# Clearing the sign on ScalarE instead of VectorE in a weight conversion, with the clamp's bounds in the other order

## The chip, the cores and the metric

One Trainium2 chip, one of its cores. The metric is the device time of one execution in microseconds. A profile of one execution gives the instruction times used below. In it PE is TensorE (PEld its weight loads), DVE is VectorE, ACT is ScalarE, POOL is GpSimd and SP is SyncE, whose queue issues the DMAs. Each engine works off one list of instructions in its order, so an instruction that waits holds up all that stand behind it on that engine.

## What is computed

A recurrence over 768 time steps for 4 x 8 heads of size 40, and then two gated feed-forward layers over the 3072 rows that it gives. Cut to what matters here:

```python
for t in range(S):                                   # S = 768
    y[:, :, t] = einsum('bhd,bhde->bhe', rt, state)
    Sa = einsum('bhde,bhe->bhd', state, at)
    state = state * wt[:, :, None, :] - einsum('bhd,bhe->bhde', Sa, bt) + einsum('bhd,bhe->bhde', vt, kt)
x = y.transpose(0, 2, 1, 3).reshape(3072, 320)
g = x @ w_gate;  x = (g * sigmoid(g) * (x @ w_val)) @ w_out          # layer 1
out = (sigmoid(x @ w2_gate) * (x @ w2_val)) @ w2_out                  # layer 2
```

The six weight matrices (320 x 1536 or 1536 x 320) come to the kernel as 64-bit floats. Their conversion to a pair of 32-bit floats, a high part and a rest, is what is changed.

## The kernel before

**The attention part** (`attention`, lines 43 to 677) takes the time axis in 12 chunks of 64 steps. For each chunk `prep_a` builds scaled keys, `prep_b` solves small triangular systems on VectorE (lines 409 to 423) with a round trip through DRAM, and `chain` and `post` carry the state on and form the output. Several chunks are in work at once; `merge` interleaves these generators by rates and due times written at lines 635 to 645.

**The feed-forward part** (`Ffn`) cuts the hidden size of 1536 into 12 slices of 128 (index f). For one slice `load_w` converts the weights and `gate` uses them: 16 TensorE matmuls per block of 256 rows (line 809), a sigmoid on ScalarE (813), one or two products on VectorE (815, 816), the split of the result into a rounded high part on ScalarE (817) and a rest on GpSimd (818); `add` then makes 6 matmuls more (827). The rows come in 12 blocks.

**The order of the stages.** Some slices of layer 1 are converted and used while attention still runs (`more` and `extra`, lines 1016 to 1041). After attention the remaining slices of layer 1 run over all blocks, and during that time the 12 slices of layer 2 are converted (`load_w2`, called from `each1`, line 1081). Then layer 2 runs from weights that are all there. The program's text is not the order on the engines: the kernel is built with `schedule_with_timeline_sim=True` (line 1186), so a planner writes each engine's order from its own estimate of when each instruction is ready.

**One conversion** (`load_w`, lines 699 to 736) is done three times for a slice (twice with 384 columns, once with 320), 72 times in all. A DMA brings the 64-bit words into `raw`, of which `lo` and `hi` are the even and odd 32-bit words, so both are read with a step of 8 bytes. The steps on `dt` (called `t` in the code) and `ds` (`sg`):

- 707, VectorE: `dt` = `hi` without its sign bit
- 708, GpSimd: clamp of `dt` as a 32-bit float
- 711 and 712, VectorE: two shifts, then sign and top bit of `hi` put back
- 716 and 717, VectorE: scale from the exponent bits, then times `lo`
- 727, ScalarE: rounded high part of the weight
- 729, GpSimd: `dt` minus the high part; 731, 733 or 735, GpSimd: plus `ds`, into the low part

While attention runs there is at first one `raw`, one `dt` and one `ds`; in its last chunks a second set joins, and after it there are three `raw` and two each of `dt` and `ds`.

Of the kernel before, what the change touches and what calls it, by code (L numbers as in the profile page):

```python
# [9 lines left out]
F32 = mybir.dt.float32  # L10
# [3 lines left out]
AF = mybir.ActivationFunctionType  # L14
ALU = mybir.AluOpType
# [23 lines left out]
F_LOW = 2.0**-15  # L39
F_HIGH = (1.875 - 2.0**-23) * 2.0**16  # L40
# [639 lines left out]
class Ffn:  # L680
# [7 lines left out]
    def load_w(self, pool, tag, layer, f):  # L688

        nc = self.nc  # L690
        w8 = pool.tile([P, 11 * P + 2 * DM], F32R, tag=tag, name="w8")
        wh, wl = w8[:, 0 : 6 * P + DM], w8[:, 6 * P + DM :]
        for n in range(3):
            sz = 3 * P if n < 2 else DM
            at = 3 * P * n
            (p0, t0), (p1, t1), (p2, t2) = self.raw[self.n % len(self.raw)]
            self.n += 1
            raw = p0.tile([P, 3 * P, 2], I32, tag=t0, name="raw")
            nc.sync.dma_start(
                out=raw[:, 0:sz].rearrange("p f w -> p (f w)"), in_=layer[0][f, :, 2 * at : 2 * at + 2 * sz]  # L700
            )
            lo, hi = raw[:, 0:sz, 0], raw[:, 0:sz, 1]
            t = p1.tile([P, 3 * P], I32, tag=t1, name="dt")[:, 0:sz]
            sg = p2.tile([P, 3 * P], I32, tag=t2, name="ds")[:, 0:sz]
            ts = nc.vector.tensor_scalar

            ts(out=t, in0=hi, scalar1=0x7FFFFFFF, scalar2=None, op0=ALU.bitwise_and)  # L707
            nc.gpsimd.tensor_scalar(  # L708
                out=t.bitcast(F32), in0=t.bitcast(F32), scalar1=F_LOW, scalar2=F_HIGH, op0=ALU.max, op1=ALU.min
            )  # L710
            ts(out=t, in0=t, scalar1=5, scalar2=2, op0=ALU.logical_shift_left, op1=ALU.logical_shift_right)  # L711
            nc.vector.scalar_tensor_tensor(  # L712
                out=t, in0=hi, scalar=-(1 << 30), in1=t, op0=ALU.bitwise_and, op1=ALU.bitwise_or
            )

            ts(out=sg, in0=t, scalar1=-(1 << 23), scalar2=None, op0=ALU.bitwise_and)
            nc.vector.scalar_tensor_tensor(  # L717
                out=sg.bitcast(F32),
                in0=lo.bitcast(U32),
                scalar=2.0**-52,  # L720
                in1=sg.bitcast(F32),
                op0=ALU.mult,
                op1=ALU.mult,
            )
            tf, pf = t.bitcast(F32), sg.bitcast(F32)
            w = wh[:, at : at + sz]
            nc.scalar.copy(out=w, in_=tf)  # L727
            sub = nc.gpsimd.tensor_tensor
            sub(out=tf, in0=tf, in1=w.bitcast(F32), op=ALU.subtract)  # L729
            if n < 2:  # L730
                sub(out=wl[:, 2 * P * n : 2 * P * n + 2 * P], in0=tf[:, 0 : 2 * P], in1=pf[:, 0 : 2 * P], op=ALU.add)
                g = slice(64 * n, 64 * n + 64)
                sub(out=wl[g, 4 * P : 5 * P], in0=tf[g, 2 * P :], in1=pf[g, 2 * P :], op=ALU.add)
            else:
                sub(out=wl[:, 5 * P :], in0=tf, in1=pf, op=ALU.add)
            yield
        self.w = wh, wl
# [452 lines left out]
```

## Time and profile before

| | |
|---|---|
| time, median of 3 runs | 1460.96 us (1457.96 to 1463.65) |
| span of the profiled execution | 1462.6 us |
| busy share of the span | PE 88%, PEld 83%, DVE 59%, ACT 37%, POOL 46% |
| granted TensorE clock, mean | 0.890 of full speed |
| ending chain, by engine | PE 43%, DVE 30%, DMA 10%, POOL 5%, SP's queue 5%, issue 5%, ACT 1% |

The page gives the profiled execution by its span alone. The span lies within the three timed runs, 0.1% above their median, so a difference worked out in the span is applied to the median as it stands. The busy share says how much of the span an engine was executing, not whether the end waited for it. The chain is followed back from the last instruction, at each step to what released it; its shares say what the end waited for.

### The profile page before, as it was taken

The page shows a single profiled execution, that of the slowest core. Times are in us where ns is not written, and L with a number is a line of the kernel's source. Part 1 is how long each engine was busy: PE and PEld are TensorE (multiplying, and loading weights), DVE is VectorE, ACT ScalarE, POOL GpSimd, SP SyncE. Part 2 cuts the span into 40 slices and gives each one's busy share as a digit, 9 for nine tenths or more (in the row PEclk, how much of TensorE's full clock was granted, in tenths as well). Part 3 has the DMA queues.
Part 4 walks back from the last instruction along what each step waited for, and adds up shares of the span by engine and source line. Part 5 has one row for each costly group of instructions (what it writes and reads, how often), then busy time and mean ns, then how long its engine had stood idle before and what let it go on. Part 6 is the DMA issues. An engine that isn't in the chain of part 4 may idle for free.

```text
span 1462.6 us, 32637 instructions
## 1 busy us (share of the span) xinstructions
PE 1282.7 (88%) x13197; PEld 1207.8 (83%) x13197; DVE 858.1 (59%) x1644; ACT 535.1 (37%) x1260; POOL 678.0 (46%) x800
## 2 busy tenths in 40 slices
PE   4548867789899899887979999999999999999996
PEld 4447756678888888786979988889999999999996
DVE  8679759388756865876687999886311122112111
ACT  5223524253445444533433332333333333333331
POOL 4378468352213222245587888996222222222221
PEclk7556858696989999886999999999999999999998
DMA  5854884946355446425234654442100000100000
GB/s 139 206 114 107 170 195 94 187 97 159 88 125 140 102 119 147 93 62 132 87 99 155 185 164 132 140 135 95 63 21 21 21 21 22 30 21 21 12 13 17
DMA packets 242096, 144.49 MB, mean 99 GB/s; under 512 B 186768, under 2 KB 218512, under 8 KB 241552
## 3 DMA queue, kind: packets, MB, share of 16 engines
q1 hardware_dynamic: 241936, 142.31, 37.6%
q8 instruction: 106, 1.74, 0.5%
q14 instruction: 54, 0.44, 0.1%
HBM read 104.00 MB, written 38.27 MB: 97 GB/s over the span
## 4 chain that ended last, share of the span: by engine, by line
PE 43%; DVE 30%; DMA 10%; POOL 5%; SPq 5%; issue 5%; ACT 1%; POOLq 0%; DVEq 0%; ACTq 0%
PE g L809 21%; PE po L827 11%; DVE pr L417 7%; PE gv L809 4%; DVE part L423 4%; DMA sn<-nd 3%; DVE dt L712 3%; DVE dt L711 2%; POOL dt L708 2%; SPq L219 2%; DVE ds L717 2%; DMA raw<-in_w_dram 2%; DVE g L815 1%; PE kps L364 1%; DVE dt L707 1%
## 5 line engine op out<-in xcount | busy, mean ns | idle before, releaser
L809 PE MATMUL g<-x,w 128*128 128x256 f32 x3552 | 495.3, 284 | 12.8 <-DVE g L815 11.8
L809 PEld LDWEIGHTS g<-x,w 128*128 128x128 f32 x3552 | 462.8, 190 | 19.0 <-DVE g L815 16.7
L818 POOL TENSOR_TENSOR hl<-g,hh 128x256 fp32r<-128x256 f32 x288 | 220.5, 768 | 452.8 <-ACT hh L817 409.5
L816 DVE TENSOR_TENSOR g<-g,g 128x256 f32<-128x256 f32 x222 | 93.7, 422 | 307.7 <-PE g L809 297.7
L827 PE MATMUL po<-w,hh 128*128 128x320 f32 x1152 | 230.0, 314 | 2.8 <-ACT hh L817 1.4
L817 ACT CAST hh<-g 128x256 fp32r<-128x256 f32 x288 | 117.0, 406 | 302.8 <-DVE g L816 276.4
L809 PE MATMUL gv<-x,w 128*128 128x256 f32 x1056 | 173.4, 318 | 30.4 <-DVE g L816 18.2
L809 PEld LDWEIGHTS gv<-x,w 128*128 128x128 f32 x1056 | 152.9, 217 | 38.2 <-DVE g L816 24.2
L827 PEld LDWEIGHTS po<-w,hh 128*128 128x128 f32 x1152 | 179.0, 191 | 4.6 <-ACT hh L817 2.6
L417 DVE TENSOR_TENSOR pr<-part,sn 128x4 f32<-128x4 f32 (+4 forms) x180 | 150.1, 834 | 4.0
L827 PE MATMUL po<-w,hl 128*128 128x320 f32 x576 | 145.1, 318 | 2.9 <-POOL hl L818 2.9
L813 ACT ACTIVATE g<-g 128x256 f32<-128x256 f32 x222 | 85.1, 384 | 142.5 <-PE g L809 109.4
L708 POOL TENSOR_SCALAR dt<-dt 128x384 f32<-128x384 f32 (+1 forms) x72 | 109.2, 1519 | 40.9 <-DVE dt L707 38.0
L729 POOL TENSOR_TENSOR dt<-dt,w 128x384 f32<-128x384 f32 (+1 forms) x72 | 79.3, 1101 | 78.4 <-ACT w L727 32.3
L827 PEld LDWEIGHTS po<-w,hl 128*128 128x128 f32 x576 | 93.8, 191 | 5.2 <-POOL hl L818 4.2
L423 DVE TENSOR_REDUCE part<-pr 128x2 f32<-128x4 f32 (+4 forms) x180 | 88.9, 494 | 4.0
L364 PE MATMUL kps<-lq,kbt 104*128 104x128 f32 x384 | 69.4, 338 | 18.6 <-DVE lq L374 15.6
L364 PEld LDWEIGHTS kps<-lq,kbt 104*128 104x128 f32 x384 | 61.8, 244 | 23.2 <-issue 13.2
L727 ACT CAST w<-dt 128x384 fp32r<-128x384 f32 (+1 forms) x72 | 35.6, 495 | 98.6 <-DVE dt L712 91.5
L570 PE MATMUL aps<-rbd,ut 104*128 104x128 f32 x384 | 61.5, 307 | 9.3 <-DVE ysb L607 3.0
L707 DVE TENSOR_SCALAR dt<-raw 128x384 int32<-128x384 int32 (+1 forms) x72 | 44.9, 624 | 40.2 <-DMA raw<-in_w_dram 34.1
L372 ACT ACTIVATE bn<-kps 64x256 f32<-64x256 f32 x96 | 36.4, 379 | 84.5 <-PE kps L364 46.6
(129 smaller groups left out, 1762.1 us busy)
## 6 DMA issues: line engine op xcount, KB each, us to landing
raw<-in_w_dram SPq DMA_DIRECT2D x48, 384.0 KB
xd<-x SPq DMA_DIRECT2D x12, 896.0 KB
x<-xd SPq DMA_DIRECT2D x12, 896.0 KB
raw<-in_w_dram SPq DMA_DIRECT2D x24, 320.0 KB
pn<-pd SPq DMA_DIRECT2D x46, 160.0 KB
ld<-in_a_kb_dram SPq DMA_DIRECT2D x22, 320.0 KB
ld<-rd SPq DMA_DIRECT2D x44, 160.0 KB
sn<-nd SPq DMA_DIRECT2D x24, 256.0 KB
```

What stands on the lines that cost most here:

```text
L364: nc.tensor.matmul(kps[:, n].rearrange("p h t -> p (h t)"), lhsT=kbt[0:PW, n, :], rhs=lq[m % 3][0:PW, 4 * g4 + n].rearrange("p h t -> p (h ...
L417: nc.vector.tensor_tensor(out=o, in0=xs[:, 0:kk, None, 0:n].to_broadcast([P, kk, 2, n]), in1=sn[:, None, 0:n, n : n + 2].rearrange("p o s ...
L423: nc.vector.tensor_reduce(out=xs[:, 0:kk, n : n + 2], in_=o, axis=AX.X, op=ALU.add)
L570: nc.tensor.matmul(aps[:, n, h2], lhsT=ut[0:PW, x, 2 * h2 : 2 * h2 + 2].rearrange("p u s -> p (u s)"), rhs=rbd[0:PW, x, h2].rearrange("p b ...
L708: nc.gpsimd.tensor_scalar(out=t.bitcast(F32), in0=t.bitcast(F32), scalar1=F_LOW, scalar2=F_HIGH, op0=ALU.max, op1=ALU.min)
L729: sub(out=tf, in0=tf, in1=w.bitcast(F32), op=ALU.subtract)
L809: nc.tensor.matmul(gv[n], lhsT=p, rhs=q, start=e == 0, stop=e == len(seq) - 1)
L813: nc.scalar.activation(out=g, in_=gv[0], func=AF.Sigmoid)
L816: nc.vector.tensor_tensor(out=g, in0=gv[1], in1=g, op=ALU.mult)
L817: nc.scalar.copy(out=hh, in_=g)
L818: self.heng.tensor_tensor(out=hl, in0=g, in1=hh.bitcast(F32), op=ALU.subtract)
L827: self.nc.tensor.matmul(ops[u], lhsT=p[:, us], rhs=q, start=first and n == 0, stop=last and n == 2)
```

## The change

One line of the conversion and the arguments of the next are altered:

```diff
-            ts(out=t, in0=hi, scalar1=0x7FFFFFFF, scalar2=None, op0=ALU.bitwise_and)
+            nc.scalar.activation(out=t.bitcast(F32), in_=raw.bitcast(F32)[:, 0:sz, 1], func=AF.Abs)
             nc.gpsimd.tensor_scalar(
-                out=t.bitcast(F32), in0=t.bitcast(F32), scalar1=F_LOW, scalar2=F_HIGH, op0=ALU.max, op1=ALU.min
+                out=t.bitcast(F32), in0=t.bitcast(F32), scalar1=F_HIGH, scalar2=F_LOW, op0=ALU.min, op1=ALU.max
             )
```

`ts` is VectorE's `tensor_scalar`. The sign of `hi` is now cleared by an absolute value on ScalarE, which reads the same 32-bit words as floats, with the same step, and writes the same tile. The clamp on GpSimd has the same two operations on the same data in the other order. Nothing else of the text changes; the planner writes the order on the engines anew.

## Rows read from the trace of the kernel before

**Rows 1.** The page of the profile, its head.

```profile
span 1462.6 us, 32637 instructions
```

**Rows 2.** Stretches: us, each engine's busy us (instructions), granted TensorE clock, DMA share, GB/s.

```profile
0.00:330.00 330.00, 224.74 (x2623) 196.96 (x2624) 242.75 (x428) 126.91 (x266) 188.59 (x211) 0.69 0.64 145
...
620.00:720.00 100.00, 87.27 (x1218) 78.13 (x1213) 62.08 (x127) 36.58 (x85) 46.34 (x55) 0.83 0.36 88
720.00:860.00 140.00, 127.46 (x1155) 120.92 (x1155) 122.56 (x261) 46.44 (x118) 111.51 (x122) 1.00 0.46 146
860.00:1005.00 145.00, 132.77 (x996) 128.37 (x995) 130.16 (x230) 45.74 (x116) 131.23 (x141) 0.99 0.42 137
1005.00:1462.60 457.60, 445.90 (x3517) 444.86 (x3515) 96.15 (x219) 146.36 (x375) 126.11 (x185) 0.99 0.09 26
```

**Rows 3.** Waits of TensorE, 860 to 1005 us: total us, times, longest.

```profile
PE g L809 <- DVE g L815: 10.4, 11, 2.0
PE po L827 <- POOL hl L818: 1.7, 3, 0.6
```

**Rows 4.** The chain of waits, by line: 0:330, 620:720, 720:860, 860:1005, in that order.

```profile
by line: DVE pr L417 12.0%; SPq L219 7.8%; DMA sn<-nd 5.9%; DVE part L423 5.4%; issue 5.0%; DMA pn<-pd 3.5%; PE gv L809 3.1%; DVE lq L374 2.8%; DVE wp L183 2.8%; DMA ld<-in_a_kb_dram 2.4%; DMA raw<-in_w_dram 2.4%; SPq L443 2.0%; DMA pd<-wp 
...
by line: PE gv L809 13.3%; DVE pr L417 9.8%; DMA raw<-in_w_dram 9.6%; DVE part L423 6.6%; PE po L827 5.9%; DMA xs<-ob 4.6%; DMA xd<-part 4.5%; DMA sn<-nd 4.2%; PE yps L596 4.0%; DMA nd<-bn 3.7%; issue 3.4%; PE aps L570 3.1%; DVE dt L707 2.3
...
by line: issue 10.7%; DVE dt L712 7.9%; DVE dt L711 7.1%; DVE wacc L1115 6.5%; DVE g L815 5.5%; POOL dt L708 5.3%; DVE g L816 5.3%; DVE ds L717 5.2%; DMA wt<-in_a_w_dram 5.2%; DVE wacc L1114 5.1%; POOL dt L729 4.7%; DVE dt L707 4.2%; DMA ra
...
by line: DVE dt L712 14.5%; issue 14.4%; POOL dt L708 10.5%; DVE dt L711 9.8%; DVE ds L717 6.9%; POOL hl L818 5.8%; DVE g L815 5.3%; DVE dt L707 5.1%; DVE ds L716 5.1%; POOL dt L729 4.8%; POOL w L731 4.6%; DVE g L816 4.2%; POOL w L733 2.9%;
```

**Rows 5.** Stretches as in group 2, for line 707 alone.

```profile
0.00:330.00 330.00, 5.95 (x15) 0.69 0.64 145
...
620.00:720.00 100.00, 4.57 (x9) 0.83 0.36 88
720.00:860.00 140.00, 11.78 (x22) 1.00 0.46 146
860.00:1005.00 145.00, 21.53 (x25) 0.99 0.42 137
```

**Rows 6.** Line 707, whole span: durations ns min/median/max; its waits; who waited for it.

```profile
L707 DVE TENSOR_SCALAR dt<-raw x72: 309/411/2056, 84.2 to 999.5; 128x384 int32<-128x384 int32 x48, 128x320 int32<-128x320 int32 x24
...
  DMA raw<-in_w_dram: 34.1, 12
...
  POOL dt L708: 38.0, 38
```

**Rows 7.** VectorE, 862 to 869 us in order of time: start us, us.

```profile
863.13 2.06 DVE L707 TENSOR_SCALAR dt<-raw 128x320 int32<-128x320 int32 x1
...
866.08 0.36 DVE L707 TENSOR_SCALAR dt<-raw 128x384 int32<-128x384 int32 x1
866.93 0.62 DVE L711 TENSOR_SCALAR dt<-dt 128x320 int32<-128x320 int32 x1 [0.49 <-POOL dt L708]
```

**Rows 8.** GpSimd in the same stretch.

```profile
863.57 0.73 POOL L818 TENSOR_TENSOR hl<-g,hh 128x256 fp32r<-128x256 f32 x1
864.27 0.73 POOL L731 TENSOR_TENSOR w<-dt,ds 128x256 fp32r<-128x256 f32 x1
```

**Rows 9.** ScalarE groups by shape: xcount, busy us, mean ns, idle before.

```profile
L727 ACT CAST w<-dt 128x384 fp32r<-128x384 f32 x48 | 24.6, 512 | 64.2 <-DVE dt L712 57.2 <-PE yps L596 5.1 <-POOL w L735 1.8
...
L465 ACT COPY zt<-zps 32x512 f32<-32x512 f32 x24 | 14.9, 619 | 18.5 <-PE zps L455 18.2
...
L427 ACT COPY xt<-part 128x512 f32<-128x512 f32 x12 | 13.2, 1103 | 11.4 <-DVE part L423 11.4
...
L81 ACT ACT_TABLE_LOAD x1 | 1.3, 1283 | 0.8 <-PEq L1178 0.8
L813 ACT ACT_TABLE_LOAD x1 | 1.3, 1283 | 0.0
```

**Rows 10.** What line 813 waited for on ScalarE, 860 to 1005 us.

```profile
  POOL hl L818: 20.8, 18
```

## The prediction

> **What bounds the kernel now.** The profiled execution spans 1462.6 us [rows 1]. I read the busy times by stretch first [rows 2]. From 1005 us on TensorE is busy 445.9 of 457.6 us: layer 2 is a pure TensorE stage, has no conversions, and nothing of this change can reach it. From 720 to 1005 us TensorE is busy 260.2 of 285 us (127.46 + 132.77) at a granted clock of 0.99 to 1.00, while VectorE is busy 252.7 us and GpSimd 242.7 us of the same 285. All three are nearly full, and what TensorE loses there is 24.8 us. The waits of TensorE in the last 145 us name the cause: it stands for VectorE's line 815, and a little for GpSimd's 818, 12.1 us in all [rows 3]. Before 720 us the picture is that of attention: TensorE has gaps everywhere, and the chain goes through the triangular solves on VectorE and through DMAs [rows 4].
>
> Line 707 was read next. Of its 72 runs 47 lie between 720 and 1005 us, and there it takes 33.3 us of VectorE; 9 lie in 620 to 720 us (4.6 us) and 15 before 330 us (6.0 us) [rows 5]. Its duration is uneven: 309 ns at best, 411 in the median, 2056 at worst [rows 6]. In the busiest stretch the mean is 21.53 / 25 = 0.86 us [rows 5]. Then the chain of waits by stretch [rows 4]: line 707 has 2.3% of 100 us, 4.2% of 140 us and 5.1% of 145 us, which is 2.3 + 5.9 + 7.4 = 15.6 us of the way to the end. That is 41% of the 37.9 us for which it is busy in these three stretches. In the first 330 us it is not among the lines listed, so under 2.0%, or 6.6 us; I leave it out of the sum.
>
> **What the change removes.** 72 VectorE instructions, of which 15.6 us stand on the chain. If nothing took their place, that is the gain. But some of the length of line 707 is not its own work. A clean run over 384 columns took 0.36 us, while one over 320 columns took 2.06 us; during it GpSimd ran lines 818 and 731, and line 707 ended 0.2 us after the second of them [rows 7, 8]. So part of what is measured as line 707 is time in which it stood beside GpSimd. The next VectorE instruction on SBUF data, 711 or 712, may stand in its place. With clean runs alone, 56 x 0.36 us = 20.2 us of the 37.9 us would be freed, and by the same 41% the chain loses 8.3 us, not 15.6.
>
> The Trainium skill bears on that (GPSIMD Engine Reference, section "Key points"): GpSimd shares its SBUF interfaces with VectorE and collides with VectorE instructions in a two-port mode or with two SBUF inputs. The trace agrees as far as the stretched run goes. By that rule the lost time goes to the next such VectorE instruction, and the gain is the smaller of the two figures above.
>
> **What it adds.** 72 absolute values on ScalarE. The trace has none. The nearest row is the cast of the same tile, 128 x 384, at 512 ns [rows 9]; it reads without a step, while the new one reads every second word. A ScalarE copy with a step of two words on its output (32 x 512) took 619 ns, one that reads with a step of 32 words (128 x 512) took 1103 ns [rows 9]. Scaled by columns the last is 1103 x 384 / 512 = 827 ns. So the bounds are 512 and 827 ns; I take 512, because a step of two words is nearer to the 619 ns row, which is hardly above what the cast gives for 512 columns (512 x 512 / 384 = 683 ns). In all 72 x 0.51 = 37 us of ScalarE, at most 60. ScalarE is busy 46.4 of 140 and 45.7 of 145 us [rows 2], so 47 of them, 24 to 39 us, fit into 193 idle us.
>
> Where the clamp on GpSimd waits for the cleared word, the new instruction stands on the path: 38 of 72 times today [rows 6]. Of the 56 conversions in the three stretches that makes 30, and by the same 41% 12.3 are on the chain: 12.3 x 0.51 = 6.3 us come back, or 10.2 us at 827 ns.
>
> The Trainium skill speaks against the change (ScalarE: Activation LUTs, "Rules for kernel authors"): simple elementwise work belongs on VectorE, which is faster per element. For the clean runs the trace agrees, 0.36 against 0.51 us; the runs beside GpSimd at a mean of 0.86 us go the other way. By the rule alone each conversion becomes 0.15 us longer, by the stretched rows it becomes shorter.
>
> **What it moves.** Line 707 is the first to touch `raw`, and VectorE stood 34.1 us in 12 waits for its DMA [rows 6]. In the chain that DMA has 2.4% of 330 us and 9.6% of 100 us, 7.9 + 9.6 = 17.5 us [rows 4]. These waits go to ScalarE's list. VectorE is then free for its solves (417, 423), but held up instead are ScalarE's copies of transposed tiles and sigmoids (360, 349, 813, 817), for which TensorE waits. Line 711 still needs the whole way over DMA, ScalarE and GpSimd. So the bounds are a gain of 17.5 us (what is on the chain vanishes) and a loss of 34.1 - 17.5 = 16.6 us (what was harmless on VectorE gets onto the path on ScalarE). I take zero, between the two. The new instruction also has to wait until GpSimd has let go of the previous `dt`. No DMA is added; the release of `raw` still hangs on line 717. The other order of the clamp is two operations for two, and costs nothing: GpSimd passes over the same columns in one instruction.
>
> **The sum.** -15.6 + 6.3 + 0 = -9.3 us against the span of 1462.6 us [rows 1], or against the median: 1460.96 - 9.3 = 1451.7. I predict 1452 us.
>
> **The rivals.** About 0.5% (7.3 us) is what a measurement of this kernel can tell from no change: its three runs spread over 5.7 us.
>
> *GpSimd keeps the pace.* From 860 to 1005 us it is busy 131.2 of 145 us [rows 2], its load is unchanged, and the sigmoid already waits 20.8 us for its line 818 [rows 10]. Then relieving VectorE only turns VectorE's work into VectorE's idle time. With the smaller relief of 8.3 us and 6.3 us coming back, the gain is 2.0 us, and with a little off in the earlier stretch some 3: 1458 us. Against it: GpSimd had 13.8 us idle there, so it is not quite full.
>
> *ScalarE is held up (the slower one).* The waits for `raw` and for the previous `dt` block ScalarE in front of the copies and sigmoids that TensorE needs. It costs up to 16.6 us; with the 9.3 us of gain lost too, and about two thirds of the wait effective, 11 us: 1472. It decides where ScalarE waits more than some 25 us for `raw`, and TensorE's waits for ScalarE grow by half of that. For it: 15 conversions fall in the first 330 us, where the buffers are single. Against it: ScalarE is a small part of the chain there, VectorE a large one [rows 4].
>
> *The moved wait pays.* VectorE's solves no longer stand behind a late DMA, and over half of the 17.5 us is won on top: -9.3 - 9.7 = -19 us, 1442. What TensorE loses after 720 us, 24.8 us, leaves room for the first term; the second lies before it.
>
> *Activation tables are switched.* A load took 1283 ns, and there are two in the whole span, one at the start and one at the first sigmoid [rows 9]; so copies and sigmoids live side by side. If the absolute value did not, each conversion would cost up to two loads, 72 x 2 x 1.28 = 185 us, 1646. No run here shows an absolute value beside a sigmoid. The Trainium skill (ScalarE: Activation LUTs, "Table sets: the hidden batching unit") has it in every set, and so no further load.
>
> A thing without a price of its own is the planner's new order. That the order is not the text's can be seen: the next conversion's 707 stands ahead of this one's 711 [rows 7]. It can shift any of the cases by some us, and widens the range.
>
> **How the numbers follow.** Chances: the forecast (-9.3, from -4 to -16) 0.42; GpSimd's pace 0.27; ScalarE held up 0.18; the moved wait pays 0.12; tables 0.01. The predicted time is that of the first. Faster by over 0.5%: about three quarters of the first (0.31), all of the fourth (0.12) and a little of the second (0.03), together 0.46. Slower by over 0.5%: most of the third (0.16), the tables (0.01) and the second with a bad order (0.03), 0.20. The rest is 0.34. The range must hold the first, second and fourth and half of the third: from 1436, the fourth with some order luck, to 1468. The forecast's own range is 1445 to 1457.
>
> **What would show it.** Right: VectorE's busy time falls by 35 to 45 us, and ScalarE's rises by 36 to 42 us; a new ScalarE group of 72 with a mean near 0.5 us; two table loads; TensorE's idle time from 720 us to the end of the conversions falls from 24.8 us by 7 to 10; GpSimd's time is as before. Wrong: 711, 712, 716 and 717 grow longer by what 707 had too much (the wait was handed on); ScalarE shows long waits for `raw`, and TensorE waits for 360, 349 or 817 (ScalarE is held up); the mean of the new group is near 0.8 us or above; the stretch up to 720 us, where I let nothing change, moves by more than 5 us.

## The result, and the profile after

The changed kernel takes 1440.63 us in the median of 4 runs (1434.55 to 1442.74); the kernel before, run beside it, 1460.28 us (1457.96 to 1463.65). The ratio is 0.9871, 95% interval 0.9845 to 0.9897: 19.7 us faster. The forecast of 1452 us had the right sign and its range of 1436 to 1468 held the time, but the gain is more than twice the 9.3 us of its sum.

The page of the profile after, its head and busy times (compare the table of before and [rows 1]); before, the same lines gave DVE 858.1, ACT 535.1 and POOL 678.0 us:

```profile
span 1439.6 us, 32705 instructions
...
PE 1256.0 (87%) x13197; PEld 1187.5 (82%) x13197; DVE 827.8 (58%) x1572; ACT 566.9 (39%) x1332; POOL 599.6 (42%) x800
```

VectorE lost 30.3 us, ScalarE gained 31.8 us; both ways were foreseen, each with somewhat more (35 to 45, 36 to 42 us). GpSimd lost 78.4 us; that was not. The groups by shape show where, ScalarE's new instruction and its tables first, then GpSimd's clamp (line, operation, tiles, count, busy us, mean ns, idle before and its releasers):

```profile
L707 ACT ACTIVATE dt<-raw 128x384 f32<-128x384 f32 x48 | 26.7, 556 | 36.9 <-DMA raw<-in_w_dram 30.9 <-POOL w L733 2.9 <-POOL w L735 2.9
L707 ACT ACTIVATE dt<-raw 128x320 f32<-128x320 f32 x24 | 11.9, 496 | 16.0 <-DMA raw<-in_w_dram 13.4 <-POOL w L733 2.5
...
L81 ACT ACT_TABLE_LOAD x1 | 1.3, 1283 | 0.8 <-PEq L1178 0.8
L813 ACT ACT_TABLE_LOAD x1 | 1.3, 1283 | 0.0
```

```profile
L708 POOL TENSOR_SCALAR dt<-dt 128x384 f32<-128x384 f32 x48 | 27.1, 565 | 38.1 <-ACT dt L707 31.6 <-DMA xd<-x 5.7 <-PE gv L809 0.7
L708 POOL TENSOR_SCALAR dt<-dt 128x320 f32<-128x320 f32 x24 | 12.8, 532 | 20.4 <-ACT dt L707 17.9 <-DVE g L815 2.5
```

The same two groups of the clamp before:

```profile
L708 POOL TENSOR_SCALAR dt<-dt 128x384 f32<-128x384 f32 x48 | 77.3, 1612 | 28.7 <-DVE dt L707 28.7
L708 POOL TENSOR_SCALAR dt<-dt 128x320 f32<-128x320 f32 x24 | 32.0, 1334 | 12.2 <-DVE dt L707 9.3 <-DVE part L423 2.6
```

The clamp fell from 1612 to 565 ns at 384 columns, and from 109.3 to 39.9 us in all; that the order of its two operations does this is shown by the experiments below. The stretches of after, with the columns of [rows 2]:

```profile
0.00:330.00 330.00, 214.86 (x2657) 188.21 (x2658) 237.80 (x409) 131.42 (x275) 165.88 (x212) 0.72 0.64 148
620.00:720.00 100.00, 87.97 (x1311) 80.71 (x1310) 69.50 (x136) 45.52 (x106) 46.41 (x65) 0.91 0.40 106
720.00:860.00 140.00, 127.38 (x1103) 121.83 (x1102) 117.72 (x249) 57.05 (x143) 100.08 (x136) 0.99 0.50 155
860.00:1005.00 145.00, 141.95 (x1097) 139.54 (x1096) 109.02 (x196) 54.90 (x140) 98.63 (x127) 1.00 0.40 129
```

From 860 to 1005 us GpSimd has 98.6 us of work where it had 131.2, and TensorE loses 3.1 us where it lost 12.2. (In the changed kernel the conversions end at 970 us; the 3.1 us all lie before that.) From 720 to 860 us TensorE is as busy as before, 127.4 us, although GpSimd has 11 us less to do: something there eats the gain. From both stretches together TensorE's idle time fell from 24.8 to 15.7 us. Attention, too, ended earlier: its last output (line 607) came at 747.4 us instead of 761.8, the last conversion (735) at 969.4 instead of 1006.3, the last sum of layer 1 (1094) at 1023.1 instead of 1046.4. The lines for attention and layer 1, before and then after, with the first and the last start:

```profile
L607 DVE TENSOR_TENSOR ysb<-yps,pn x24: 205/215/217, 129.3 to 761.8; 128x64 f32<-128x64 f32 x24
L1094 DVE TENSOR_TENSOR part<-po,part x24: 473/480/492, 832.6 to 1046.4; 128x320 f32<-128x320 f32 x24
```

```profile
L607 DVE TENSOR_TENSOR ysb<-yps,pn x24: 208/214/229, 131.6 to 747.4; 128x64 f32<-128x64 f32 x24
L1094 DVE TENSOR_TENSOR part<-po,part x24: 479/481/492, 821.5 to 1023.1; 128x320 f32<-128x320 f32 x24
```

In these two executions some 14 us were won before the end of attention and 9 after it. The sixteen profiles of this case (before, after and all experiments below but the clamps by themselves) put the weight the other way. The end of attention hardly goes by the clamp: it comes at 745.4 to 762.4 us in the nine kernels with max first and at 742.7 to 755.2 us in the seven with min first, 4 us apart in the mean. The stretch from there to the last sum of layer 1 does: 280.4 to 292.4 us against 261.7 to 275.7 us, 15 us apart in the mean. These kernels differ in other edits too, but most of what goes with the short clamp lies after attention.

What the sigmoid waits for on ScalarE, 860 to 1005 us, which was 20.8 us for line 818 in [rows 10], and then the chain of waits of 720:860 and of 860:1005, as in [rows 4]:

```profile
  POOL hl L818: 2.4, 3
```

```profile
by line: DMA wt<-in_a_w_dram 19.2%; PE g L809 10.1%; issue 8.6%; DVE ds L717 7.2%; PE gv L809 6.1%; DVE dt L712 5.9%; PE po L827 5.4%; DVE wacc L1115 5.2%; DVE g L815 4.4%; DVE g L816 4.3%; DVE ds L716 3.7%; DVE wacc L1114 3.5%; DVE dt L711
...
by line: PE g L809 31.3%; PE po L827 13.6%; DVE dt L712 9.1%; issue 7.8%; DVE ds L717 7.3%; DVE dt L711 6.5%; DVE ds L716 5.7%; DVE g L815 5.6%; DVE g L816 3.8%; DVE part L1094 2.1%; POOL w L731 1.2%; POOL dt L729 1.1%; POOL dt L708 1.0%; P
```

In the second stretch the clamp (708) went from 10.5% of the chain to 1.0%, and TensorE's own matmuls (809, 827) took its place. In the first, the largest item is now the DMA of `wt` with 19.2% (26.9 us), which was 5.2% before. `wt` belongs to a guard that looks whether the decay input is in range: 24 loads (line 1110) with two reductions each on VectorE (1114, 1115), spread over the start of layer 1's stage. The change does not touch it.

### The profile page after: what moved, and what is told of

It reads as the page before. It is cut to its first block, busy times and chain, and to the rows that moved or that the text cites. A ratio compares the mean times of both kernels' runs of the same rounds, so it can differ in the third digit from the quotient of the medians.

```text
span 1439.6 us, 32705 instructions
## 1 busy us (share of the span) xinstructions
PE 1256.0 (87%) x13197; PEld 1187.5 (82%) x13197; DVE 827.8 (58%) x1572; ACT 566.9 (39%) x1332; POOL 599.6 (42%) x800
## 4 chain that ended last, share of the span: by engine, by line
PE 47%; DVE 27%; DMA 11%; SPq 5%; issue 4%; ACT 3%; POOL 2%; DVEq 0%; ACTq 0%; POOLq 0%
PE g L809 24%; PE po L827 12%; DVE pr L417 7%; DVE part L423 4%; PE gv L809 4%; DMA raw<-in_w_dram 2%; DVE ds L717 2%; DMA sn<-nd 2%; DVE dt L712 2%; DMA wt<-in_a_w_dram 2%; PE kps L364 2%; PE tp L304 2%; DVE g L815 1%; DVE ds L716 1%; DVE g L816 1%
## 5 line engine op out<-in xcount | busy, mean ns | idle before, releaser
L809 PE MATMUL gv<-x,w 128*128 128x256 f32 x1056 | 167.9, 312 | 31.6 <-POOL w L733 9.4
L809 PEld LDWEIGHTS gv<-x,w 128*128 128x128 f32 x1056 | 149.7, 212 | 37.2 <-DVE g L816 16.2
L417 DVE TENSOR_TENSOR pr<-part,sn 128x4 f32<-128x4 f32 (+4 forms) x180 | 154.0, 856 | 4.0
L374 DVE TENSOR_TENSOR lq<-kps,part 64x256 f32<-64x256 f32 x96 | 40.5, 422 | 44.1 <-ACT bn L372 42.4
L304 PE MATMUL tp<-ident,part 128*104 128x128 f32 x288 | 51.4, 316 | 15.1 <-POOL part L322 7.0
L708 POOL TENSOR_SCALAR dt<-dt 128x384 f32<-128x384 f32 (+1 forms) x72 | 39.9, 554 | 58.5 <-ACT dt L707 49.5
```

The lines of the kernel that those rows point to most:

```text
L304: nc.tensor.transpose(ps[0 : x.shape[1], n, :], x, ident)
L417: nc.vector.tensor_tensor(out=o, in0=xs[:, 0:kk, None, 0:n].to_broadcast([P, kk, 2, n]), in1=sn[:, None, 0:n, n : n + 2].rearrange("p o s ...
L809: nc.tensor.matmul(gv[n], lhsT=p, rhs=q, start=e == 0, stop=e == len(seq) - 1)
```

## The experiments

The theory after the result: the clamp's order is the whole gain, and moving the sign clearing is worth little. The rival: the move gives the 9.3 us forecast, and the clamp the rest.

**The two edits one at a time, and the clamp by itself.**

`e1_and_minfirst`, the clamp's edit alone:

```diff
-  out=t.bitcast(F32), in0=t.bitcast(F32), scalar1=F_LOW, scalar2=F_HIGH, op0=ALU.max, op1=ALU.min
+  out=t.bitcast(F32), in0=t.bitcast(F32), scalar1=F_HIGH, scalar2=F_LOW, op0=ALU.min, op1=ALU.max
```

> Only the clamp's bounds are swapped; the sign is still cleared on VectorE, and the order of the instructions on every engine is that of before. Theory A (the clamp alone is the gain: upper bound first runs about 1 us shorter on GpSimd): line 708 falls from 1519 ns to about 550 ns, GpSimd's busy time by about 69 us, and the time is 1440 to 1447 us. Theory B (the move to ScalarE is the gain, and the clamp is short in the changed kernel because VectorE leaves GpSimd alone): line 708 stays near 1500 ns and the time within 0.3% of before, 1456 to 1464. Theory C (each gives a part): line 708 near 550 ns, 1447 to 1454 us.

`e2_abs_maxfirst`, the move alone:

```diff
-  ts(out=t, in0=hi, scalar1=0x7FFFFFFF, scalar2=None, op0=ALU.bitwise_and)
+  nc.scalar.activation(out=t.bitcast(F32), in_=raw.bitcast(F32)[:, 0:sz, 1], func=AF.Abs)
```

> The absolute value on ScalarE with the clamp as before, lower bound first; the order on every engine is that of the changed kernel. Theory A: line 708 is back at about 1500 ns, GpSimd is as busy as before (670 to 690 us), and the time is 1455 to 1468 us: the move alone is worth nothing or costs a little. Theory B: line 708 near 550 ns, 1438 to 1444 us. Theory C: 708 at 1500 ns, 1447 to 1455 us, which is what the prediction had for the whole change (1452).

`e3_clamps`, only clamps on GpSimd, six of each kind, with both layers and attention left out (VectorE only adds up the clamped tiles, 5.6 us in all):

```diff
+  nc.gpsimd.tensor_scalar(out=ca, in0=src, scalar1=LOW, scalar2=HIGH, op0=ALU.max, op1=ALU.min)
+  nc.gpsimd.tensor_scalar(out=cb, in0=src, scalar1=HIGH, scalar2=LOW, op0=ALU.min, op1=ALU.max)
+  # cc, cd: the same two on zeros; ce, cf: the same two with the scalars exchanged; cg, ch: max alone, min alone
```

> Clamps alone on GpSimd, 128 x 384 floats, six of each, with VectorE idle; the layers are left out and the output is a sum of the clamped tiles. On the weights' words: lower bound first, then upper bound first; the same two on zeros; max with the upper bound then min with the lower; min with the lower then max with the upper; max alone; min alone. If the order of the operations sets the time: about 1490 ns wherever max is first with min second, about 500 ns wherever min is first, zeros or not. If the data or the scalars set it: the two with swapped scalars or those on zeros differ from the first two. If contention with VectorE made the long clamp, all two-operation clamps take about the same here.

Measured: e1 1437.85 us, ratio 0.9867 (0.9836 to 0.9898); e2 1466.86 us, ratio 1.0073 (1.005 to 1.0096). The clamp alone gives all of the change's gain (0.9871), somewhat below the 1440 to 1447 us expected of it, and the move alone costs 0.7% (0.0073 x 1454.64, the median of before beside it, is 11 us). The groups of e3 on GpSimd:

```profile
L40 POOL TENSOR_SCALAR ce<-src 128x384 f32<-128x384 f32 x6 | 9.1, 1521 | 0.0
L36 POOL TENSOR_SCALAR cc<-z 128x384 f32<-128x384 f32 x6 | 9.0, 1496 | 0.1
L32 POOL TENSOR_SCALAR ca<-src 128x384 f32<-128x384 f32 x6 | 8.9, 1487 | 1.7 <-ACT src L22 1.7
L44 POOL TENSOR_SCALAR cg<-src 128x384 f32<-128x384 f32 x6 | 7.2, 1203 | 0.0
L46 POOL TENSOR_SCALAR ch<-src 128x384 f32<-128x384 f32 x6 | 7.0, 1164 | 0.1
L34 POOL TENSOR_SCALAR cb<-src 128x384 f32<-128x384 f32 x6 | 3.0, 506 | 0.0
L42 POOL TENSOR_SCALAR cf<-src 128x384 f32<-128x384 f32 x6 | 3.0, 500 | 0.0
L38 POOL TENSOR_SCALAR cd<-z 128x384 f32<-128x384 f32 x6 | 3.0, 500 | 0.0
```

Max first takes 1487 to 1521 ns, min first 500 to 506 ns, on the same data, on zeros (`z`) and with the bounds exchanged (`ce`, `cf`), with next to nothing running beside it. So the order of the operations sets the time. Line 711 of e2 and of e1 shows what VectorE did with its free time (idle before it, by releaser; before, it waited 21.1 us for 708):

```profile
L711 DVE TENSOR_SCALAR dt<-dt 128x384 int32<-128x384 int32 (+1 forms) x72 | 51.3, 713 | 41.0 <-POOL dt L708 40.9
```

```profile
L711 DVE TENSOR_SCALAR dt<-dt 128x384 int32<-128x384 int32 (+1 forms) x72 | 39.7, 552 | 5.2 <-POOL dt L708 5.0
```

VectorE is 22.5 us less busy in e2 (835.6 of 858.1) and waits 19.8 us longer for the long clamp: the freed time became idle time. That is the rival in which GpSimd keeps the pace. It does not explain a loss.

**Where the move costs 0.7%.** First theory: it helps in attention and harms in layer 1's stage, where ScalarE is held up; then moving only layer 2's conversions harms, only layer 1's helps. Four kernels, the sign on ScalarE for one layer's 36 conversions (`g1` and `g2` with the long clamp, `g3` and `g4` with the short one):

```diff
+  if layer[1]:        # g1, g3: layer 1 alone; g2, g4: "if not layer[1]"
+      nc.scalar.activation(out=t.bitcast(F32), in_=raw.bitcast(F32)[:, 0:sz, 1], func=AF.Abs)
+  else:
       ts(out=t, in0=hi, scalar1=0x7FFFFFFF, scalar2=None, op0=ALU.bitwise_and)
```

> Clamp as before, lower bound first. The absolute value on ScalarE only for the 36 conversions of layer 1, most of them while attention runs; layer 2's keep VectorE. Theory S (the move helps in attention and harms while layer 2's weights are converted beside layer 1): attention ends about 3 us earlier than before and the stretch behind it is as before, so 0.1 to 0.4% faster, about 1451 us in a call whose before is at 1455. Theory H (waiting for raw holds up ScalarE's copies for TensorE): attention ends later, 0.3% or more slower. Theory P (the planner's new order moves the time by itself, without regard to the place): anything within 1% either way, with no relation to the next run.

> Clamp as before. The absolute value on ScalarE only for layer 2's 36 conversions. Theory S: attention as before, the stretch from its end to the end of layer 1 is about 6 us longer, 0.3 to 0.9% slower than before; VectorE's line 815 waits longer for the sigmoid 813, which stands behind the absolute value on ScalarE. Theory H: as before within 0.2%. The prediction's mechanism (a shorter chain on VectorE): 0.6% faster, since 13 of its 15.6 us lie here.

> As the first of this call, with the short clamp. Theory S: the best of all, some 3 to 5 us below the kernel with only the clamp swapped, ratio to before 0.983 to 0.986. Theory P: anything within 1% of that kernel.

> As the second of this call, with the short clamp. Theory S: the worst of the four short-clamp kernels, 3 to 6 us above the one with only the clamp swapped, ratio 0.988 to 0.992. The prediction's mechanism: below it, 0.980 to 0.984.

Measured, against 1455.57 us: g1 1466.35, 1.0076 (1.0046 to 1.0106); g2 1453.99, 0.9996 (0.9975 to 1.0017); g3 1437.91, 0.9886 (0.985 to 0.9921); g4 1433.89, 0.9865 (0.9835 to 0.9895). The theory fell: the loss comes with layer 1's half. Nor does g1's profile show ScalarE held up: its last absolute value runs at 774 us, and the time that TensorE loses below lies after it. The stretch 780 to 860 us of before, e2 and g1, columns as in [rows 2]:

```profile
780.00:860.00 80.00, 76.76 (x578) 73.36 (x577) 68.97 (x165) 26.40 (x67) 60.26 (x67) 1.00 0.56 178
```

```profile
780.00:860.00 80.00, 70.47 (x517) 67.12 (x517) 66.78 (x151) 30.34 (x75) 61.85 (x70) 0.98 0.54 166
```

```profile
780.00:860.00 80.00, 71.25 (x527) 68.30 (x527) 67.75 (x159) 24.17 (x62) 60.89 (x68) 0.98 0.56 178
```

TensorE does 6.3 and 5.5 us less in these 80 us; call this the hole. From the end of attention to the last sum of layer 1 it is 290.5 us in e2 and 284.6 us before, 5.9 us more; that is about half of the 11 us, and where the other half lies these single executions don't show. The chain of 720:860 in e2 points to a line:

```profile
by line: DMA wt<-in_a_w_dram 20.9%; issue 14.6%; POOL dt L708 8.4%; DVE dt L712 7.6%; DVE wacc L1115 4.8%; DVE ds L717 4.6%; PE gv L809 4.2%; DVE ds L716 4.1%; DVE g L816 4.1%; DVE dt L711 3.3%; DVE g L815 3.3%; DVE wacc L1114 3.2%; POOL hl
```

The DMA of `wt` is 20.9% of 140 us, 29.3 us, against 7.3 us before. Over all kernels so far its share of that chain sorts them: 5.2% (before), 8.9% (e1), 5.2% (g2) and 7.1% (g4), whose TensorE is busy 75.2 to 76.8 us of the 80; 20.9% (e2), 16.8% (g1), 17.1% (g3) and 19.2% (the change), with 70.5 to 72.0 us. VectorE's list in e2 shows what stands where:

```profile
792.54 0.42 DVE L816 TENSOR_TENSOR g<-gv,g 128x256 f32<-128x256 f32 x1
793.38 0.60 DVE L711 TENSOR_SCALAR dt<-dt 128x384 int32<-128x384 int32 x1 [0.42 <-POOL dt L708]
794.82 0.49 DVE L1114 TENSOR_REDUCE wacc<-wt 128x1 f32<-128x320 f32 x1 [0.83 <-DMA wt<-in_a_w_dram]
795.22 0.48 DVE L1115 TENSOR_REDUCE wacc<-wt 128x1 f32<-128x320 f32 x1
795.61 0.55 DVE L712 SCALAR_TENSOR_TENSOR dt<-raw,dt 128x384 int32<-128x384 int32 x1
796.08 0.48 DVE L1114 TENSOR_REDUCE wacc<-wt 128x1 f32<-128x320 f32 x1
796.47 0.48 DVE L1115 TENSOR_REDUCE wacc<-wt 128x1 f32<-128x320 f32 x1
796.87 0.42 DVE L815 TENSOR_TENSOR g<-gv,g 128x256 f32<-128x256 f32 x1
797.70 0.42 DVE L816 TENSOR_TENSOR g<-gv,g 128x256 f32<-128x256 f32 x1
```

Line 816 of one gate ends at 793.0 us. Before the next gate's 815 at 796.9, the list has a wait for the clamp, 711, a wait for a load of `wt`, two pairs of reductions and 712; TensorE then stands 2.33 us for line 816, its longest wait in the stretch. But the same instructions stand in the same order between two gates of before, without a wait and one gate later (behind the last gate that reads `gv`, where e2 has them ahead of it):

```profile
800.42 0.42 DVE L816 TENSOR_TENSOR g<-g,g 128x256 f32<-128x256 f32 x1
800.77 0.60 DVE L711 TENSOR_SCALAR dt<-dt 128x384 int32<-128x384 int32 x1
801.28 0.47 DVE L1114 TENSOR_REDUCE wacc<-wt 128x1 f32<-128x320 f32 x1
...
803.81 0.41 DVE L815 TENSOR_TENSOR g<-g,g 128x256 f32<-128x256 f32 x1
```

So reductions between the gates are not new; that VectorE stands there for the loads is. Its waits for `wt` from 720 to 1005 us (us, times, longest), before and in e2:

```profile
DVE wacc L1114 <- DMA wt<-in_a_w_dram: 1.4, 2, 1.0
```

```profile
DVE wacc L1114 <- DMA wt<-in_a_w_dram: 4.7, 6, 1.3
```

There are six such waits in the change, g1 and g3 too (4.8, 4.6 and 5.7 us), and two to four in e1, g2 and g4 (2.2, 2.2 and 4.5 us). Second theory, from here: the planner, given other instructions, starts the guard beside gates where its loads have not landed, and that is the loss.

**The guard taken out, and no sign clearing at all.** `k1` and `k2` leave the 24 loads and 48 reductions of the guard out (`k1` is otherwise before, `k2` is e2). `m1` and `m2` clear no sign on any engine and let the clamp read `raw` directly (long and short), so a negative weight becomes the lower bound; they relieve VectorE with no instruction put elsewhere:

```diff
-                if f in (2, 6, 10):      # k1, k2
+                if False:
```

```diff
-  ts(out=t, in0=hi, scalar1=0x7FFFFFFF, scalar2=None, op0=ALU.bitwise_and)      # m1, m2
-  out=t.bitcast(F32), in0=t.bitcast(F32), ...
+  out=t.bitcast(F32), in0=raw.bitcast(F32)[:, 0:sz, 1], ...
```

> Before, with the 24 loads of wt and their 48 reductions on VectorE (lines 1110, 1114, 1115) left out; the flag that they set is set as if they had passed, so the guard against decays outside the bounds is left out. Base for the next run; VectorE loses 22.7 us of work between 790 and 860 us. Some 0.2 to 0.5% faster than before if that work stood on the path.

> The absolute value on ScalarE with the long clamp, and the same guard left out. Theory W (the move alone lost its 0.7% because the planner put the loads of wt where VectorE waits for them, 4.7 us in 6 waits against 1.4 in 2): within 0.2% of the run before this one, or faster. Theory H (ScalarE's own list is held up by the absolute value) or theory P (the rest of the new order): still 0.5 to 0.9% slower than the run before this one.

> Before without any clearing of the sign: line 707 is gone and no engine does its work; the long clamp reads the word from raw. Negative weights then come out as the lower bound. This is the most that freeing VectorE of line 707 can bring at the long clamp. By the prediction's chain of waits (15.6 us with nothing put back, or 8.3 us by clean runs) the ratio to before is 0.989 to 0.994. If GpSimd keeps the pace: 0.997 to 1.003. The clamp on GpSimd should keep near 1500 ns with its stepped input, else the run says less.

> The same with the short clamp, upper bound first, again with negative weights coming out as the lower bound. If VectorE's time is worth nothing here either, as with the clamp alone swapped, 0.985 to 0.988. If it is worth something once GpSimd is no longer the pace, 0.975 to 0.983.

Measured, against 1458.14 us: k1 1460.54, 1.002 (0.9999 to 1.004); k2 1459.81, 1.0009 (0.9985 to 1.0032); m1 1456.85, 0.9987 (0.9969 to 1.0005); m2 1433.51, 0.9835 (0.98 to 0.987). Without the guard the move costs nothing, and gains nothing (k2 against k1). All absolute values are in k2, so ScalarE's list is not the loss. k1 was expected 0.2 to 0.5% faster than before and is not. With the long clamp even 72 instructions less on VectorE, with nothing put in their place, gain nothing that can be told from zero; with the short clamp m2 gains 1.65%. m1 is not clean: TensorE does 68.9 us of the 80 there, less than in e2, with `wt` at 10.2% of the chain, so a gain and such a loss may lie over each other in it. And a hole in this stretch alone does not say what the whole time will be.

**The guard kept, but late.** To take the wait away and keep the whole computation, `wt` was put into the buffers of `xin`, which come free later; its reductions then run from about 830 us to 1275 us instead of 781 to 854 us. `n0`: sign on VectorE, long clamp; `n1`: the move alone; `n2`: both edits; `n3`: the clamp's edit alone:

```diff
-                        wt = y_p.tile([P, DM], F32, tag="wt", name="wt")
+                        wt = y_p.tile([P, 2, DM + 64], F32, tag="xin", name="wt")[:, 0, 0:DM]
```

> Before, with the guard kept but its 24 loads of wt put in the buffers of xin, so that they take turns with layer 2's inputs: all its reductions on VectorE come after the first blocks of layer 1, most in layer 2, where VectorE is idle. Base for the next run. Leaving the guard out altogether made no difference (1.002), so 0.998 to 1.003 of before.

> The same with the absolute value on ScalarE and the long clamp. Theory W (the move alone loses 0.7% by the place of the guard's reductions at the start of the layer 1 stage, where TensorE lost 5 us more than before between 780 and 860 us): within 0.3% of the run before this one, and no hole in that stretch. Theory P (the rest of the order, or ScalarE's list): 0.5 to 0.9% slower than the run before this one.

> The changed kernel with the late guard. Theory W: 4 to 6 us below the changed kernel, ratio to before 0.982 to 0.985, because it has the hole at the start of layer 1 too. Theory P: as the changed kernel, 0.985 to 0.990.

> The clamp alone swapped, sign on VectorE, with the late guard: that kernel had no hole, so as it was, 0.985 to 0.988, or up to 0.2% less since VectorE has 22.7 us less to do beside the conversions.

Measured, against 1454.75 us: n0 1459.39, 1.0025 (1.0007 to 1.0043); n1 1456.22, 1.0005 (0.9979 to 1.003); n2 1423.18, 0.9781 (0.9747 to 0.9815); n3 1441.26, 0.9891 (0.9858 to 0.9924). The hole of 780:860 is gone in n1; and n2 keeps TensorE all but full to the end of the conversions, which n3 does not:

```profile
780.00:860.00 80.00, 75.59 (x563) 73.07 (x563) 57.03 (x108) 32.07 (x82) 68.44 (x75) 0.98 0.43 140
```

```profile
780.00:860.00 80.00, 78.55 (x603) 76.79 (x602) 65.72 (x124) 34.48 (x88) 64.24 (x82) 1.00 0.47 153
860.00:1005.00 145.00, 144.72 (x1139) 144.52 (x1138) 102.58 (x206) 56.35 (x144) 96.88 (x127) 1.00 0.42 140
```

```profile
780.00:860.00 80.00, 78.90 (x599) 76.62 (x599) 69.13 (x132) 27.13 (x72) 60.77 (x81) 1.00 0.46 155
860.00:1005.00 145.00, 141.43 (x1094) 139.55 (x1095) 117.32 (x229) 46.64 (x124) 101.69 (x132) 1.00 0.41 135
```

So with the guard late the move costs nothing (n1 against n0, whose interval lies above 1: the delay itself costs a little), and with the short clamp as well it is worth 1423.18 / 1441.26 = 0.987, 18 us by the medians and 16 us by the two ratios (the intervals of n2 and n3 lie apart). That is more than expected: n2 came out below its 0.982 to 0.985, n3 above its 0.985 to 0.988. TensorE's 860:1005 accounts for 3.3 us of it; from the end of attention to the last sum of layer 1 the two profiles differ by 7.1 us (261.7 and 268.8). n2 beats both kernels: 2.2% under before, where the change is 1.3% under it.

One run does not fit a simple account. g4 moves layer 2's half beside the short clamp, has no hole (75.2 of the 80 us), and is no faster than e1 (0.9865 against 0.9867). What the move is worth thus rests on n2 against n3, one pair of plans; every edit gives the planner a new order, and its part in the 18 us was not taken apart.

## Why the prediction was right in its sign and wrong in its size

**The step that failed** is the sentence on the clamp: two operations for two, "and costs nothing: GpSimd passes over the same columns in one instruction". It costs 1487 ns one way and 506 the other by itself (e3), and in the changed kernel the 72 clamps take 109.3 - 39.9 = 69.4 us less of GpSimd; this edit alone gives the whole gain (e1, 0.9867). So a term put at nothing was the gain. The rows of before priced one order only; with no row for the other, the edit had to carry bounds on both sides, as the absolute value did, and it got a zero. The Trainium skill (GPSIMD Engine Reference, "Elementwise — side-by-side cycle accounting") gives bodies of up to two operations 1.03 cycles per element; an estimate from it at 1.2 GHz is 384 x 1.03 / 1.2 = 330 ns and a fixed part. The 500 to 506 ns of min first leave some 170 ns for that part, a size that no run here shows; the 1487 ns of max first are far from it, and the measurement decides. Held beside the profile of before, that figure would have shown the old clamp to be too long.

**The term of -15.6 us for VectorE's line 707** fell too. A share of the chain is not a gain where another engine stands right behind: taking it off VectorE brings nothing measurable with the long clamp (k2 against k1 1459.81 / 1460.54, n1 against n0 1456.22 / 1459.39; m1, which takes all of it away, 0.9987), and in e2 19.8 of the 22.5 us freed come back as waiting for the clamp. That is the rival "GpSimd keeps the pace", and its reason, 131.2 of 145 us, was right. Its price of 1458 left out that both edits meet: the change shortens the very work that kept the pace. The whole sum of -9.3 us for the move, then, was measured as a loss: +11 us (e2).

**What the prediction put aside as some us of widening**, the planner's new order, is that loss, as far as two edits can show it: k2 (guard out) and n1 (guard late) bring it to 1.0009 and 1.0005. The changed kernel still has the hole (TensorE 72.0 of the 80 us, 76.7 in e1) and the six waits, which fits with its being no faster than e1, while with the guard late the same two edits beat the clamp alone (n2 against n3).

**Right:** the absolute value takes 556 and 496 ns, where 512 was taken between 512 and 827; two table loads, none more. The Trainium skill (ScalarE: Activation LUTs, "Table sets: the hidden batching unit") has the absolute value in every set, and the trace agrees. TensorE's idle time from 720 us to the end of the conversions fell by 9.1 us, where 7 to 10 were said; but that number came true by luck, for it is the clamp's doing: the clamp alone takes the idle time to 10.7 us (e1), the move alone to 27.2 us (e2). By the same luck the rival "the moved wait pays", with 1442 us, lies next to the time measured: e1, which moves no wait, lies near it too (1437.85 us). ScalarE did take the wait for `raw` over, and more of it than the 34.1 us of [rows 6]:

```profile
  DMA raw<-in_w_dram: 44.3, 23
  POOL w L733: 5.5, 7
  POOL w L735: 2.9, 5
  POOL dt L708: 49.5, 24
```

TensorE's waits for ScalarE stayed small all the same, 1.4 us from 720 to 1005 us (0.8 for line 817, 0.6 for 761), so neither "ScalarE is held up" nor "the moved wait pays" shows. The handing on of VectorE's stretched time was not broad: in after 711 and 712 have become shorter (668 to 579 ns, 807 to 781), 716 and 717 longer (437 to 482, 817 to 831); in e2, with the long clamp, 711 is longer (713).

**Wrong besides:** GpSimd's time was to stay as before and fell by 78.4 us. VectorE's fall, 30.3 us, missed the 35 to 45 said, and ScalarE's rise, 31.8 us, the 36 to 42, though its new group takes 38.6 us by itself. The stretch up to 720 us, where nothing was to change, moved in the single profiles (attention's last output 14.4 us earlier, 9.8 us in e1); over all profiles the two clamps are 4 us apart there.

**Still open:** why max first is slow on GpSimd was not looked into; only the times are shown. What part of the gain before 720 us goes through which wait was not tried. That VectorE waits oftener for the guard's loads is shown by the lists, and that removing or delaying the guard removes the loss is measured; but both edits also give the planner a new order, half of e2's loss is not placed, which single instruction makes the planner do it is not known, and g3 against g4 is too close to say that layer 1's half costs as much beside the short clamp.

## What to carry to other kernels

An edit that "only" reorders the operations of an instruction needs a price of its own (here, on GpSimd, nearly a factor of three): time both forms by themselves before judging a change that holds them. Work taken off one engine pays only if the next engine in the same chain has room, so cost the edits of a change together, by stage. Where a planner writes the order, look in the chain after for a line that the change doesn't touch and that has grown: here a side job's loads went from 5.2% to 19.2% of a stretch, and only with that job out of the way was the other edit worth something, 16 to 18 us in the one pair of kernels tried.

## What the runs showed of the hardware that was not expected

On GpSimd a `tensor_scalar` of 128 x 384 floats with max and then min took 1487 to 1521 ns, with min and then max 500 to 506 ns, on the weights' words as on zeros and with the bounds either way round. A single max (1203 ns) and a single min (1164 ns) took more than twice as long as the pair min and max.
